# First-chunk v transposed on TensorE, q norms summed as columns, later first-chunk weight products in the out banks, opening loads reordered

## The chip, the cores and the metric

The kernel runs on one core of a Trainium2 chip. The metric is the device time of one execution in microseconds (us). A profile is one further reading of one of the timed executions; its span is about 2 us shorter than the time told for the same execution. In the profile PE is TensorE's matmuls and PEld its weight loads, DVE is VectorE, ACT is ScalarE, POOL is GpSimd and SP is SyncE. A bank is one of the buffers in PSUM into which TensorE writes its products and from which ACT or DVE empty them. A transfer has landed when its data may be used.

## The reference

Four batches of cross-covariance attention (6016 positions, 256 channels) feed a SwiGLU block with 1536 hidden units.

```python
qn = q / (norm(q, axis=1) + 1e-6)          # norms over the 6016 positions
kn = k / (norm(k, axis=1) + 1e-6)
a  = softmax(kn.transpose(0, 2, 1) @ qn / tau)      # 256 x 256 per batch
x  = (v @ a).reshape(B * N, C)
out = (silu(x @ w_gate) * (x @ w_val)) @ w_out
```

## The kernel before

The kernel never forms `v @ a`. Per batch it multiplies the attention matrix into both weight matrices (the "weight products", twelve units of 128x512 each) and then runs v through the products. v is needed with channels on the partitions, so each chunk of 512 positions is cast to bf16 in DRAM and read back through a DMA transpose (`vT`). A chunk has twelve steps: one gate product, one value product, silu, multiply. The output products of a chunk are spread over the steps of the next chunk.

Batch 0 has nothing to hide behind. Its opening loads q and k, sums the squares, forms `k^T q`, takes the softmax, makes the first four weight products and starts chunk 0, making the other eight weight products during the first four steps.

```python
def load_v(b, ci):                       # cast to DRAM, then DMA transpose
    ...
    nc.gpsimd.dma_start(out=vb[:mv, :]..., in_=v[b, cs*P:cs*P+mv, :]...)
    vT = vpool.tile([P, CH, CS * P], BF16, tag="vT")
    nc.sync.dma_start_transpose(out=vT[:, :, :mv], in_=vb[:mv, :])

def first_norm(b, t, which):             # q squares on ACT, k squares on DVE
    ...
    for s in range(pm):                  # every row of ss is the same sum
        nc.tensor.matmul(ss, ones_bf, sq[:, s, :], ...)      # 256 columns

def wp_unit(b, u, pool=psum_m, tag="misc"):      # psum_m has ONE bank
    ps = pool.tile([P, WP], FP32, tag=tag)
    for jh in range(CH):
        nc.tensor.matmul(ps, exT[:, jh, ...], src[:, jh, cols], ...)
    # even units are emptied by ACT, odd ones by DVE
    ...

# ... loads of the opening, in the order of the queue
for g, which in order: load_qk(0, g, which)      # k two groups ahead of q
load_v(*allc[0]); load_w(0); load_v(*allc[1]); load_w(1); load_w(2)
nc.gpsimd.dma_start(out=w_out_sb, ...)
...
first_softmax(0); row_sums(0)
for u in range(NFIRST): wp_unit(0, u, psum_gv, ...)     # NFIRST = 4
for gi, (b, ci) in enumerate(allc):
    for f in range(FH):
        gv_step(b, ci, f, sv)
        if gi == 0:
            for u in range(NFIRST + 2*f, min(NFIRST + 2*f + 2, len(wp_units))):
                wp_unit(0, u)
        ...
        if f == 0 and gi + VT_AHEAD < len(allc): load_v(*allc[gi + VT_AHEAD])
```

Of the kernel before, what the change touches and what calls it, by code (L numbers as in the profile page):

```python
# [17 lines left out]
def kernel(  # L18
# [61 lines left out]
    half = const.tile([P, 2 * CH], FP32)  # L80
    minus = const.tile([P, 2 * CH], FP32)
    identf = const.tile([P, P], FP32)
    warm_bf = const.tile([P, 2 * C], BF16)
    nc.vector.memset(warm_bf, 1.0)

# [21 lines left out]
    def load_v(b, ci):  # L107
# [7 lines left out]
        nc.sync.dma_start_transpose(out=vT[:, :, :mv], in_=vb[:mv, :])  # L115
        vt_ready[(b, ci)] = vT

    def gemm1_pair(b, t):

        q_sb, k_sb = qk_tiles[b]  # L120
        if t == 0:
            kq_new = psum_kq.tile([P, CH, C], FP32, tag="kq")
            state[b, "kq"] = kq_new
        kq = state[b, "kq"]
        ps, pm = pairs[t]
        last = t == NP - 1
        for jh in range(CH):
            js = slice(jh * P, (jh + 1) * P)
            if pm == 2:
                nc.tensor.matmul(kq[:, jh, :], q_sb[:, ps:ps + 2, js],  # L130
                                 k_sb[:, ps:ps + 2, :],
                                 start=(t == 0 and jh == 0), stop=last,
                                 perf_mode=DR, skip_group_check=True)
            else:
                nc.tensor.matmul(kq[:, jh, :], q_sb[:, ps, js], k_sb[:, ps, :],
                                 start=(t == 0 and jh == 0), stop=last,
                                 skip_group_check=True)

    def first_norm(b, t, which):

        x_sb = qk_tiles[b][which]
        ps, pm = pairs[t]
        sq = sqpool.tile([P, 2, C], BF16, tag="sq%d" % which)
        if which == 0:
            nc.scalar.activation(sq[:, :pm, :], x_sb[:, ps:ps + pm, :], ACT.Square)  # L145
        else:
            nc.vector.tensor_mul(sq[:, :pm, :], x_sb[:, ps:ps + pm, :],  # L147
                                 x_sb[:, ps:ps + pm, :])
        if t == 0:
            ss_new = psum_gv.tile([P, C], FP32, tag="gv"[which])  # L150
            state[b, "ss", which] = ss_new
        ss = state[b, "ss", which]
        for s in range(pm):
            nc.tensor.matmul(ss, ones_bf, sq[:, s, :],  # L154
                             start=(t == 0 and s == 0),
                             stop=(t == NP - 1 and s == pm - 1))

    def first_inv_k(b):
        nrm = work.tile([P, C], FP32, tag="nrm")
        nc.scalar.activation(nrm, state[b, "ss", 1], ACT.Sqrt)  # L160
        ink = work.tile([P, C], FP32, tag="ink")
        nc.vector.tensor_scalar_add(ink, in0=nrm, scalar1=1e-6)
        nc.vector.reciprocal(ink, ink)
        state[b, "ink"] = ink

    def first_softmax(b):
        kq, ink = state[b, "kq"], state[b, "ink"]
        nrq = work.tile([1, C], FP32, tag="nrq")
        nc.scalar.activation(nrq, state[b, "ss", 0][0:1, :], ACT.Sqrt)
        qc = psum_m.tile([P, CH], FP32, tag="misc")  # L170
        for jh in range(CH):
            nc.tensor.matmul(qc[:, jh:jh + 1], nrq[0:1, jh * P:(jh + 1) * P],
                             ones_f[0:1, 0:1], start=True, stop=True)
        keep_warm(4)
        inq = work.tile([P, CH], FP32, tag="inq")
        s_f = work.tile([P, CH, C], FP32, tag="s_f")
        nc.vector.tensor_mul(s_f[:, 0, :], kq[:, 0, :], ink)
        nc.vector.tensor_scalar_add(inq, in0=qc, scalar1=1e-6)
        nc.vector.reciprocal(inq, inq)
        if inv_tau != 1.0:  # L180
            nc.vector.tensor_scalar_mul(inq, in0=inq, scalar1=inv_tau)
        nc.vector.tensor_mul(s_f[:, 1, :], kq[:, 1, :], ink)
        exT = attn.tile([P, CH, C], BF16, tag="exT")
        for jh in range(CH):
            nc.scalar.activation(exT[:, jh, :], s_f[:, jh, :], ACT.Exp,
                                 scale=inq[:, jh:jh + 1])
        state[b, "exT"] = exT

    def norm_acc(b, t):
        q_sb, k_sb = qk_tiles[b]  # L190
# [75 lines left out]
    def row_sums(b):  # L266
        exT = state[b, "exT"]
        rs = psum_m.tile([P, CH], FP32, tag="misc")
        for ih in range(CH):
            for jh in range(CH):  # L270
                nc.tensor.matmul(rs[:, ih:ih + 1], exT[:, jh, ih * P:(ih + 1) * P],
                                 ones_bf[:, 0:1], start=(jh == 0), stop=(jh == CH - 1))
        smr = work.tile([P, CH], FP32, tag="smr")
        nc.vector.tensor_scalar_add(smr, in0=rs, scalar1=1e-9)
        nc.vector.reciprocal(smr, smr)
        Wg = attn.tile([P, CH, DFF], BF16, tag="Wg")
        Wv = attn.tile([P, CH, DFF], BF16, tag="Wv")
        state[b, "smr"], state[b, "W"] = smr, (Wg, Wv)
# [5 lines left out]

    wp_units = [(wc, w, ih) for wc in range(NWC) for w in range(2) for ih in range(CH)]

    def wp_unit(b, u, pool=psum_m, tag="misc"):

        wc, w, ih = wp_units[u]
        exT, smr = state[b, "exT"], state[b, "smr"]  # L290
        src = (w_gate_sb, w_val_sb)[w]
        dst = state[b, "W"][w]
        cols = slice(wc * WP, (wc + 1) * WP)
        ps = pool.tile([P, WP], FP32, tag=tag)
        for jh in range(CH):
            nc.tensor.matmul(ps, exT[:, jh, ih * P:(ih + 1) * P], src[:, jh, cols],  # L296
                             start=(jh == 0), stop=(jh == CH - 1))
        if u % 2 == 0:
            nc.scalar.activation(dst[:, ih, cols], ps, ACT.Copy, scale=smr[:, ih:ih + 1])
        else:  # L300
            nc.vector.tensor_scalar_mul(dst[:, ih, cols], in0=ps, scalar1=smr[:, ih:ih + 1])

    def gv_step(b, ci, f, sv):
        cs, cm = chunks[ci]
# [14 lines left out]
    class OutStage:  # L319


        def __init__(self, b, ci, sv):
            cs, self.cm = chunks[ci]
            self.sv = sv
            self.n0 = b * N + cs * P
            self.at = 0
            self.n = self.cm * FH
            self.o_ps = None

        def emit(self, count):  # L330
            for _ in range(count):
                if self.at == self.n:
                    return
                j, f = divmod(self.at, FH)
                if f == 0 and j % 2 == 0:
                    o_new = psum_o.tile([P, 2, C], FP32, tag="o")
                    self.o_ps = o_new
                nc.tensor.matmul(self.o_ps[:, j % 2, :],  # L338
                                 self.sv[:, f, j * P:(j + 1) * P],
                                 w_out_sb[:, f, :], start=(f == 0), stop=(f == FH - 1))  # L340
                self.at += 1
                if f == FH - 1 and (j % 2 == 1 or j == self.cm - 1):
                    j0 = j - j % 2
                    m = j - j0 + 1
                    o_sb = opool.tile([P, 2, C], FP32, tag="o_sb")
                    if j0 == 0:
                        nc.scalar.copy(o_sb[:, :m, :], self.o_ps[:, :m, :])  # L347
                    else:
                        nc.vector.tensor_copy(o_sb[:, :m, :], self.o_ps[:, :m, :])  # L349
                    r0 = self.n0 + j0 * P  # L350
                    nc.sync.dma_start(
                        out=out[r0:r0 + m * P, :].rearrange("(s p) c -> p s c", p=P),
                        in_=o_sb[:, :m, :])


    LOAD0, SQ0 = 10, 22
# [35 lines left out]


    NG = len(groups)
    K_AHEAD = 2
    order = []
    for g in range(NG + K_AHEAD):
        if g < NG:
            order.append((g, 1))
        if g >= K_AHEAD:  # L400
            order.append((g - K_AHEAD, 0))
    for g, which in order:
        load_qk(0, g, which)
    load_v(*allc[0])
    load_w(0)
    load_v(*allc[1])
    load_w(1)
    load_w(2)
    nc.gpsimd.dma_start(out=w_out_sb, in_=moe_w_out.rearrange("(h l) d -> l h d", l=P))
    nc.gpsimd.memset(half, 0.5)  # L410
    nc.gpsimd.memset(minus, -1.0)
    make_identity(nc, identf)
    keep_warm(10)
    for g, which in order:
        gs, gm = groups[g]
        for t in range(gs // 2, (gs + gm + 1) // 2):
            first_norm(0, t, which)
            if which == 0:
                gemm1_pair(0, t)
        if which == 1 and g == NG - 1:  # L420
            first_inv_k(0)
    first_softmax(0)
    row_sums(0)
    NFIRST = 2 * CH
    for u in range(NFIRST):
        wp_unit(0, u, psum_gv, "g" if u % 2 == 0 else "v")

    prev = None
    for gi, (b, ci) in enumerate(allc):
        sv = svpool.tile([P, FH, CS * P], BF16, tag="sv")  # L430
        for f in range(FH):
            gv_step(b, ci, f, sv)
            if gi == 0:
                for u in range(NFIRST + 2 * f, min(NFIRST + 2 * f + 2, len(wp_units))):
                    wp_unit(0, u)
            if prev is not None:
                prev.emit(prev.cm)
            if b + 1 < B:
# [40 lines left out]
```

## Time and profile before

| | before |
|---|---|
| time, first three runs | 837.96 us median, 834.86 to 839.70 |
| profiled run | 839.74 us, span 837.6 us |
| first gate product (step 0) | 46.54 us |
| step 4 (weight products done) | 63.50 us |
| chunk 1 starts | 70.41 us |

The page of the kernel before: engine, busy time, share of the span, instructions; then the TensorE clock that was granted, in tenths, for 40 equal slices of the span.

```profile
PE 807.1 (96%) x4919; PEld 489.7 (58%) x5006; DVE 550.0 (66%) x860; ACT 463.9 (55%) x827; POOL 89.9 (11%) x171
...
PEclk9959999999999999999999999999999999999999
```

TensorE is busy for 96% of the span. The idle time and the one slice at half clock both lie in the first 64 us, so that is where a change can find something.

The chain of waits of the kernel before, in order of time: start, length, what.

```profile
25.91 9.58 DMA vb<-in_v_dram
...
35.51 10.98 DMA vT<-vb
...
46.54 1.01 PE g_ps L313 x2
```

The chain goes through the load of v (landed 35.5 us) and its transpose (landed 46.5 us) to the first gate product.

The TensorE timeline of the kernel before from there: start, length, engine, line, operation, in brackets the idle time before it and what ended it.

```profile
46.54 1.01 PE L313 MATMUL g_ps<-vT,Wg 128*128 128x512 bf16 x2 [5.86 <-DMA vT<-vb]
47.34 1.06 PE L313 MATMUL v_ps<-vT,Wv 128*128 128x512 bf16 x2
48.20 1.06 PE L296 MATMUL ps<-w_gate_sb,exT 128*128 128x512 bf16 x2
50.03 1.01 PE L296 MATMUL ps<-w_gate_sb,exT 128*128 128x512 bf16 x2 [0.78 <-ACT Wg L299]
```

TensorE idled 5.86 us for the first vT. After that two matmuls of 512 columns take about 0.86 us from start to start (47.34 to 48.20), and a second weight product waits 0.78 us until ACT has emptied the only misc bank.

The table of windows of the kernel before: stretch; its length, busy time and instructions of PE; then of PEld, DVE, ACT and POOL; the granted clock; DMA share; GB/s.

```profile
20.00:30.00 10.00, 6.97 (x46) 4.78 (x46) 4.86 (x8) 4.14 (x9) 4.26 (x8) 1.00 1.12 106
...
44.00:46.00 2.00, 0.00 (x0) 0.00 (x0) 0.00 (x0) 0.00 (x0) 0.53 (x1) 0.82 1.34 179
46.00:48.00 2.00, 1.46 (x4) 0.54 (x4) 0.00 (x0) 0.41 (x1) 0.53 (x1) 0.50 1.35 183
48.00:52.00 4.00, 3.22 (x8) 0.99 (x7) 1.44 (x2) 0.94 (x3) 0.10 (x1) 0.50 1.27 189
...
60.00:64.00 4.00, 3.22 (x10) 1.15 (x10) 1.51 (x3) 1.28 (x2) 1.28 (x3) 0.71 1.10 145
```

The clock falls to half inside the wait and is back only between 60 and 64 us.

### The profile page before, as it was taken

What the parts mean: (1) busy time and instruction counts of PE and PEld (TensorE: products, weight loads), DVE (VectorE), ACT (ScalarE), POOL (GpSimd) and SP (SyncE); (2) the same over time, 40 slices, a digit from 0 to 9 for tenths busy, and PEclk for the clock granted to TensorE, in tenths of its full rate; (3) what the DMA queues carried; (4) which work ended last, traced back from release to release, by engine and by line L of the source; (5) the groups of instructions that cost most, each with busy time, mean ns of one, the idle gap of its engine ahead of it and who ended that gap; (6) DMA issues with size and microseconds to landing.
All of it is one profiled execution on the core that took longest, in us unless ns stands there. A gap on an engine that the chain in (4) does not pass through costs nothing.

```text
span 837.6 us, 13474 instructions
## 1 busy us (share of the span) xinstructions
PE 807.1 (96%) x4919; PEld 489.7 (58%) x5006; DVE 550.0 (66%) x860; ACT 463.9 (55%) x827; POOL 89.9 (11%) x171
## 2 busy tenths in 40 slices
PE   7769999999999999999999999999999999999998
PEld 4425566565565656666566556666556566566566
DVE  4526788867655688867565688876755555555554
ACT  3625777645555677755545567764554544544543
POOL 5523000024300000013320000003100000000000
PEclk9959999999999999999999999999999999999999
DMA  9999621129982111217993121114931212112101
GB/s 88 147 160 125 103 64 39 51 51 153 147 133 58 41 49 39 58 47 122 134 147 78 45 62 40 51 39 85 175 70 47 51 51 64 39 51 64 42 31 58
DMA packets 93874, 64.85 MB, mean 77 GB/s; under 512 B 53616, under 2 KB 93040, under 8 KB 93040
## 3 DMA queue, kind: packets, MB, share of 16 engines
q0 software_dynamic: 18544, 27.01, 25.4%
q1 hardware_dynamic: 75264, 36.97, 18.9%
q8 instruction: 39, 0.64, 0.3%
q14 instruction: 27, 0.22, 0.1%
HBM read 78.64 MB, written 36.96 MB: 138 GB/s over the span
## 4 chain that ended last, share of the span: by engine, by line
PE 90%; DMA 5%; issue 1%; ACT 1%; DVE 1%; POOL 1%; DVEq 0%; ACTq 0%; POOLq 0%
PE o_new L338 29%; PE v_ps L313 29%; PE g_ps L313 27%; PE ps L296 3%; DMA k_sb<-in_k_dram 2%; PE kq_new L130 2%; DMA vT<-vb 1%; DMA vb<-in_v_dram 1%; ACT sq L194 1%; DVE sv L317 1%; DVE acc_new L203 1%; POOL k_sb L103 0%; PE cs L211 0%; ACT silu L316 0%; POOL q_sb L103 0%
## 5 line engine op out<-in xcount | busy, mean ns | idle before, releaser
L317 DVE TENSOR_TENSOR sv<-silu,v_ps 128x512 bf16<-128x512 bf16 (+1 forms) x576 | 382.5, 673 | 229.3 <-ACT silu L316 217.4
L316 ACT ACTIVATE silu<-g_ps 128x512 bf16<-128x512 f32 (+1 forms) x576 | 337.5, 587 | 316.7 <-PE g_ps L313 263.4
L338 PE MATMUL o_new<-w_out_sb,sv 128*128 128x256 bf16 x2256 | 338.5, 273 | 1.6
L313 PE MATMUL v_ps<-vT,Wv 128*128 128x512 bf16 (+1 forms) x1120 | 332.4, 376 | 5.8 <-DVE sv L317 3.0
L313 PE MATMUL g_ps<-vT,Wg 128*128 128x512 bf16 (+1 forms) x1101 | 329.1, 377 | 6.0 <-DMA vT<-vb 5.9
L338 PEld LDWEIGHTS <-sv 128*128 128x128 bf16 x2256 | 220.7, 98 | 140.8
L313 PEld LDWEIGHTS <-Wv 128*128 128x128 bf16 x1152 | 113.1, 98 | 136.2 <-issue 7.6
L313 PEld LDWEIGHTS <-Wg 128*128 128x128 bf16 x1152 | 107.4, 98 | 34.6 <-issue 7.8
L203 DVE TENSOR_TENSOR acc_new<-acc_new,sq 128x512 f32<-128x512 f32 x135 | 93.3, 691 | 23.6 <-ACT sq L194 21.1
L194 ACT ACTIVATE sq<-q_sb 128x512 bf16<-128x512 fp8e5 x72 | 44.3, 615 | 0.0
L194 ACT ACTIVATE sq<-k_sb 128x512 bf16<-128x512 fp8e5 x72 | 44.1, 612 | 0.0
L130 PE MATMUL kq_new<-k_sb,q_sb 128*128 128x512 fp8e5 x184 | 42.6, 313 | 0.0
L215 POOL TENSOR_TENSOR inv<-inv,half 128x4 f32<-128x4 f32 x3 | 3.1, 1036 | 360.5 <-DVE inv L214 360.5
L347 ACT COPY o_sb<-o_new 128x512 f32<-128x512 f32 x48 | 28.1, 585 | 14.0 <-PE o_new L338 13.7
L349 DVE COPY o_sb<-o_new 128x512 f32<-128x512 f32 (+1 forms) x48 | 31.7, 661 | 3.0 <-PE o_new L338 3.0
L103 POOL DMA_DIRECT2D q_sb<-in_q_dram x48 | 26.0, 541 | 38.7 <-DMA q_sb<-in_q_dram 14.6
L103 POOL DMA_DIRECT2D k_sb<-in_k_dram x48 | 25.7, 536 | 40.3 <-DMA q_sb<-in_q_dram 18.6
L111 POOL DMA_DIRECT2D vb<-in_v_dram x48 | 24.1, 505 | 24.2 <-DMA k_sb<-in_k_dram 15.3
L154 PE MATMUL ss_new<-sq,ones_bf 128*128 128x256 bf16 x94 | 18.3, 276 | 7.8 <-DVE sq L147 5.4
L147 DVE TENSOR_TENSOR sq<-k_sb 128x512 bf16<-128x512 fp8e5 (+1 forms) x24 | 15.2, 677 | 15.1 <-DMA k_sb<-in_k_dram 15.0
L145 ACT ACTIVATE sq<-q_sb 128x512 bf16<-128x512 fp8e5 (+1 forms) x24 | 13.3, 611 | 18.5 <-DMA q_sb<-in_q_dram 14.6
L130 PEld LDWEIGHTS <-q_sb 128*128 128x256 fp8e5 x184 | 22.6, 136 | 1.1
(60 smaller groups left out, 151.5 us busy)
## 6 DMA issues: line engine op xcount, KB each, us to landing
out_dram<-o_sb SPq DMA_DIRECT2D x92, 256.0 KB, 2.4
vb<-in_v_dram POOLq DMA_DIRECT2D x44, 256.0 KB, 10.7
k_sb<-in_k_dram POOLq DMA_DIRECT2D x44, 128.0 KB, 11.2
q_sb<-in_q_dram POOLq DMA_DIRECT2D x44, 128.0 KB, 11.3
w_gate_sb<-in_moe_w_gate_dram POOLq DMA_DIRECT2D x3, 256.0 KB, 9.7
w_val_sb<-in_moe_w_val_dram POOLq DMA_DIRECT2D x3, 256.0 KB, 10.0
vT<-vb SPq DMA_TRANSPOSE x48, 3.4
w_out_sb<-in_moe_w_out_dram POOLq DMA_DIRECT2D x1, 768.0 KB, 15.8
```

The lines of the kernel that those rows point to most:

```text
L103: nc.gpsimd.dma_start(out=dst[:, gs:gs + gm, :], in_=src[b].rearrange("(p s) c -> p s c", s=NS)[:, gs:gs + gm, :])
L111: nc.gpsimd.dma_start(out=vb[:mv, :].rearrange("(p s) c -> p (s c)", s=cm), in_=v[b, cs * P:cs * P + mv, :].rearrange("(p s) c -> p (s c)" ...
L130: nc.tensor.matmul(kq[:, jh, :], q_sb[:, ps:ps + 2, js], k_sb[:, ps:ps + 2, :], start=(t == 0 and jh == 0), stop=last, perf_mode=DR, skip_ ...
L194: nc.scalar.activation(sq[:, :pm, which, :], qk_tiles[b][which][:, ps:ps + pm, :], ACT.Square)
L203: nc.vector.tensor_add(acc, acc, sq[:, s, :, :])
L296: nc.tensor.matmul(ps, exT[:, jh, ih * P:(ih + 1) * P], src[:, jh, cols], start=(jh == 0), stop=(jh == CH - 1))
L313: nc.tensor.matmul(dst[:, :mv], W[:, kk, fs], vT[:, kk, :mv], start=(kk == 0), stop=(kk == CH - 1))
L316: nc.scalar.activation(silu[:, :mv], g_ps[:, :mv], ACT.Silu)
L317: nc.vector.tensor_mul(sv[:, f, :mv], silu[:, :mv], v_ps[:, :mv])
L338: nc.tensor.matmul(self.o_ps[:, j % 2, :], self.sv[:, f, j * P:(j + 1) * P], w_out_sb[:, f, :], start=(f == 0), stop=(f == FH - 1))
L347: nc.scalar.copy(o_sb[:, :m, :], self.o_ps[:, :m, :])
L349: nc.vector.tensor_copy(o_sb[:, :m, :], self.o_ps[:, :m, :])
```

## The change

The intent is to take the wait away and to tighten the opening:

1. Chunk 0's v is loaded straight into SBUF and transposed by eight TensorE transposes during the softmax; DVE copies them out. (Chunk 0's positions are then permuted, so its output is written with another pattern.)
2. q norms are summed as columns, two one-column products per slice, so that they come out on the partitions; the last q square moves to DVE. The reciprocal of the k norms is cut into two halves, made between the last q groups.
3. The first four weight products are issued so that work starts after half of the exponentials. The other eight use the two "out" banks, idle during chunk 0, in place of the one misc bank.
4. k is loaded three groups ahead of q, not two, and both weight blocks 0 and 1 go ahead of chunk 1's v.

The diff, cut to its core:

```diff
+    def load_first_v():
+        nc.gpsimd.dma_start(
+            out=v0_sb, in_=v[0, :CS * P, :].rearrange("(p s) c -> p s c", s=CS))
+    def transpose_first_v():
+        vt_ps = psum_o.tile([P, CH, CS * P], BF16, tag="o")
+        for h in range(CH):
+            for j in range(CS):
+                nc.tensor.transpose(vt_ps[:, h, j * P:(j + 1) * P],
+                                    v0_sb[:, j, h * P:(h + 1) * P], ident)
 ...
     def first_norm(b, t, which, on_dve):
+            if which == 1:
+                nc.tensor.matmul(ss, ones_bf, sq[:, s, :], start=first, stop=last)
+            else:
+                for h in range(CH):
+                    nc.tensor.matmul(ss[:, h:h + 1], sq[:, s, h * P:(h + 1) * P],
+                                     ones_bf[:, 0:1], start=first and h == 0, stop=last, ...)
 ...
     def first_softmax(b):
-        nrq = work.tile([1, C], FP32, tag="nrq")       # root of one row,
-        ...                                            # turned by two products
+        nc.scalar.activation(inq, state[b, "ss", 0], ACT.Sqrt)
 ...
+        transpose_first_v()
+        keep_warm(4)                                   # moved down to here
+        for h in range(CH):
+            evacuate_first_v(h)
 ...
-    K_AHEAD = 2
+    K_AHEAD = 3
 ...
-    load_v(*allc[0])
+    load_first_v()
     load_w(0)
+    load_w(1)
     load_v(*allc[1])
-    load_w(1)
     load_w(2)
 ...
-                    wp_unit(0, u)
+                    wp_unit(0, u, psum_o, "o")
```

More of the change, by code (lines that the diff above doesn't have):

```diff
@@ L82 @@
     identf = const.tile([P, P], FP32)
+    ident = const.tile([P, P], BF16)
+    v0_sb = const.tile([P, CS, C], BF16)
     warm_bf = const.tile([P, 2 * C], BF16)
@@ L116, in load_v, with evacuate_first_v @@
         vt_ready[(b, ci)] = vT
+    def load_first_v():
[7 more added lines that the diff above has]
+                                    v0_sb[:, j, h * P:(h + 1) * P], ident)
+        state["vt_ps"] = vt_ps
+        vT_new = vpool.tile([P, CH, CS * P], BF16, tag="vT")
+        vt_ready[(0, 0)] = vT_new
+    def evacuate_first_v(h):
+        nc.vector.tensor_copy(vt_ready[(0, 0)][:, h, :], state["vt_ps"][:, h, :])
     def gemm1_pair(b, t):
@@ L137, in gemm1_pair, with first_norm @@
                                  skip_group_check=True)
-    def first_norm(b, t, which):
+    def first_norm(b, t, which, on_dve):
         x_sb = qk_tiles[b][which]
@@ L143, in first_norm @@
         sq = sqpool.tile([P, 2, C], BF16, tag="sq%d" % which)
-        if which == 0:
-            nc.scalar.activation(sq[:, :pm, :], x_sb[:, ps:ps + pm, :], ACT.Square)
-        else:
+        if on_dve:
             nc.vector.tensor_mul(sq[:, :pm, :], x_sb[:, ps:ps + pm, :],
                                  x_sb[:, ps:ps + pm, :])
+        else:
+            nc.scalar.activation(sq[:, :pm, :], x_sb[:, ps:ps + pm, :], ACT.Square)
         if t == 0:
-            ss_new = psum_gv.tile([P, C], FP32, tag="gv"[which])
+            ss_new = psum_gv.tile([P, CH if which == 0 else C], FP32, tag="gv"[which])
             state[b, "ss", which] = ss_new
@@ L153, in first_norm, with first_norm_k @@
         for s in range(pm):
-            nc.tensor.matmul(ss, ones_bf, sq[:, s, :],
-                             start=(t == 0 and s == 0),
-                             stop=(t == NP - 1 and s == pm - 1))
-    def first_inv_k(b):
+            first = t == 0 and s == 0
+            last = t == NP - 1 and s == pm - 1
+            if which == 1:
+                nc.tensor.matmul(ss, ones_bf, sq[:, s, :], start=first, stop=last)
+            else:
+                for h in range(CH):
+                    nc.tensor.matmul(ss[:, h:h + 1], sq[:, s, h * P:(h + 1) * P],
+                                     ones_bf[:, 0:1], start=first and h == 0, stop=last,
+                                     skip_group_check=True)
+    def first_norm_k(b):
         nrm = work.tile([P, C], FP32, tag="nrm")
@@ L162, in first_inv_k @@
         nc.vector.tensor_scalar_add(ink, in0=nrm, scalar1=1e-6)
-        nc.vector.reciprocal(ink, ink)
         state[b, "ink"] = ink
+    def first_inv_k(b, h):
+        part = state[b, "ink"][:, h * P:(h + 1) * P]
+        nc.vector.reciprocal(part, part)
     def first_softmax(b):
         kq, ink = state[b, "kq"], state[b, "ink"]
-        nrq = work.tile([1, C], FP32, tag="nrq")
-        nc.scalar.activation(nrq, state[b, "ss", 0][0:1, :], ACT.Sqrt)
-        qc = psum_m.tile([P, CH], FP32, tag="misc")
-        for jh in range(CH):
-            nc.tensor.matmul(qc[:, jh:jh + 1], nrq[0:1, jh * P:(jh + 1) * P],
-                             ones_f[0:1, 0:1], start=True, stop=True)
-        keep_warm(4)
         inq = work.tile([P, CH], FP32, tag="inq")
+        nc.scalar.activation(inq, state[b, "ss", 0], ACT.Sqrt)
         s_f = work.tile([P, CH, C], FP32, tag="s_f")
         nc.vector.tensor_mul(s_f[:, 0, :], kq[:, 0, :], ink)
-        nc.vector.tensor_scalar_add(inq, in0=qc, scalar1=1e-6)
+        nc.vector.tensor_scalar_add(inq, in0=inq, scalar1=1e-6)
         nc.vector.reciprocal(inq, inq)
@@ L182, in first_softmax @@
         nc.vector.tensor_mul(s_f[:, 1, :], kq[:, 1, :], ink)
+        transpose_first_v()
+        keep_warm(4)
+        for h in range(CH):
+            evacuate_first_v(h)
         exT = attn.tile([P, CH, C], BF16, tag="exT")
+        state[b, "exT"] = exT
+        rs = psum_m.tile([P, CH], FP32, tag="misc")
+        units = []
+        for u in range(2 * CH):
+            unit_ps = psum_gv.tile([P, WP], FP32, tag="gv"[u % 2])
+            units.append(unit_ps)
+        order = (("rs", 0), (0, 0), (1, 0), ("rs", 1), (0, 1), (1, 1),
+                 (2, 0), (2, 1), (3, 0), (3, 1))
         for jh in range(CH):
@@ L186, in first_softmax @@
                                  scale=inq[:, jh:jh + 1])
-        state[b, "exT"] = exT
+        for u, jh in order:
+            if u == "rs":
+                for ih in range(CH):
+                    nc.tensor.matmul(rs[:, ih:ih + 1], exT[:, jh, ih * P:(ih + 1) * P],
+                                     ones_bf[:, 0:1], start=(jh == 0 and ih == 0),
+                                     stop=(jh == CH - 1), skip_group_check=True)
+            else:
+                wp_matmul(b, u, jh, units[u])
+            if u == 0 and jh == 1:
+                finish_rs(b, rs)
+                wp_evacuate(b, 0, units[0])
+            elif u != "rs" and jh == 1:
+                wp_evacuate(b, u, units[u])
     def norm_acc(b, t):
@@ L272, in row_sums, with finish_rs @@
                                  ones_bf[:, 0:1], start=(jh == 0), stop=(jh == CH - 1))
+        finish_rs(b, rs)
+    def finish_rs(b, rs):
         smr = work.tile([P, CH], FP32, tag="smr")
@@ L285, with wp_matmul, wp_evacuate @@
     wp_units = [(wc, w, ih) for wc in range(NWC) for w in range(2) for ih in range(CH)]
-    def wp_unit(b, u, pool=psum_m, tag="misc"):
+    def wp_matmul(b, u, jh, ps):
         wc, w, ih = wp_units[u]
-        exT, smr = state[b, "exT"], state[b, "smr"]
-        src = (w_gate_sb, w_val_sb)[w]
+        nc.tensor.matmul(ps, state[b, "exT"][:, jh, ih * P:(ih + 1) * P],
+                         (w_gate_sb, w_val_sb)[w][:, jh, wc * WP:(wc + 1) * WP],
+                         start=(jh == 0), stop=(jh == CH - 1))
+    def wp_evacuate(b, u, ps):
+        wc, w, ih = wp_units[u]
+        smr = state[b, "smr"]
         dst = state[b, "W"][w]
         cols = slice(wc * WP, (wc + 1) * WP)
-        ps = pool.tile([P, WP], FP32, tag=tag)
-        for jh in range(CH):
-            nc.tensor.matmul(ps, exT[:, jh, ih * P:(ih + 1) * P], src[:, jh, cols],
-                             start=(jh == 0), stop=(jh == CH - 1))
         if u % 2 == 0:
@@ L301, in wp_unit @@
             nc.vector.tensor_scalar_mul(dst[:, ih, cols], in0=ps, scalar1=smr[:, ih:ih + 1])
+    def wp_unit(b, u, pool=psum_m, tag="misc"):
+        ps = pool.tile([P, WP], FP32, tag=tag)
+        for jh in range(CH):
+            wp_matmul(b, u, jh, ps)
+        wp_evacuate(b, u, ps)
     def gv_step(b, ci, f, sv):
@@ L324, in __init__ @@
             self.sv = sv
-            self.n0 = b * N + cs * P
+            pat = "(p s) c -> p s c" if (b, ci) == (0, 0) else "(s p) c -> p s c"
+            r0 = b * N + cs * P
+            self.dst = out[r0:r0 + self.cm * P, :].rearrange(pat, p=P)
             self.at = 0
@@ L349, in emit @@
                         nc.vector.tensor_copy(o_sb[:, :m, :], self.o_ps[:, :m, :])
-                    r0 = self.n0 + j0 * P
-                    nc.sync.dma_start(
-                        out=out[r0:r0 + m * P, :].rearrange("(s p) c -> p s c", p=P),
-                        in_=o_sb[:, :m, :])
+                    nc.sync.dma_start(out=self.dst[:, j0:j0 + m, :], in_=o_sb[:, :m, :])
     LOAD0, SQ0 = 10, 22
@@ L401 @@
             order.append((g - K_AHEAD, 0))
-    for g, which in order:
+    for n, (g, which) in enumerate(order):
         load_qk(0, g, which)
-    load_v(*allc[0])
+        if n == 8:
+            make_identity(nc, identf)
+            nc.gpsimd.memset(half, 0.5)
+            nc.gpsimd.memset(minus, -1.0)
+    load_first_v()
     load_w(0)
+    load_w(1)
     load_v(*allc[1])
-    load_w(1)
     load_w(2)
     nc.gpsimd.dma_start(out=w_out_sb, in_=moe_w_out.rearrange("(h l) d -> l h d", l=P))
-    nc.gpsimd.memset(half, 0.5)
-    nc.gpsimd.memset(minus, -1.0)
-    make_identity(nc, identf)
     keep_warm(10)
@@ L416 @@
         for t in range(gs // 2, (gs + gm + 1) // 2):
-            first_norm(0, t, which)
+            first_norm(0, t, which, on_dve=(which == 1 or t == NP - 1))
             if which == 0:
                 gemm1_pair(0, t)
-        if which == 1 and g == NG - 1:
-            first_inv_k(0)
+        if which == 0:
+            after_k = g - (NG - 1 - K_AHEAD)
+            if after_k == 0:
+                first_norm_k(0)
+                nc.vector.tensor_copy(ident, identf)
+            elif 1 <= after_k <= CH:
+                first_inv_k(0, after_k - 1)
     first_softmax(0)
-    row_sums(0)
     NFIRST = 2 * CH
-    for u in range(NFIRST):
-        wp_unit(0, u, psum_gv, "g" if u % 2 == 0 else "v")
     prev = None
```

## The prediction

> **What bounds the kernel now.** The page gives TensorE 96% busy and the chain of waits 90% PE; after about 64 us the kernel is a steady TensorE stream which the change leaves alone. Only the opening can move. The timeline shows it: squares, norms and q/k products until 36.2 us, softmax and the first four weight products until 40.7, then TensorE waits 5.86 us for the first vT (v landed in DRAM at 35.5; its DMA transpose took 10.98 us, to 46.5). In the table of windows the granted clock falls from 1.0 to 0.5 at about 45.6 and returns only at about 62.3. From 46.5 to 63.5 (first four steps plus eight weight products) a 512-column matmul issues every 0.43 us instead of 0.216, and TensorE also waits four times 0.78 us for ACT to empty the single misc bank. The Trainium skill (TensorE: Matmul & The Clock Gate, "What's actually happening") says that TensorE drops to half rate after an idle window of about 3.4 us; this trace agrees.
>
> **What the change does, costed.**
> 1. The first vT comes from eight PE transposes[...] and two DVE evacuations (0.6 to 0.7 each, as other 128x512 PSUM reads). They run while ACT loads the exp table (1.28 us) and computes exp (0.91), so almost nothing is added. The first gate matmul moves from 46.5 to about 40.4 us: -6.1 us.
> 2. No idle window, so no half clock. The 32 matmuls of steps 0 to 3 need 6.9 us instead of 13.7: -6.8 us.
> 3. Two out banks in place of one misc bank: four waits of 0.78 go, but the silu table load (1.28 us), hidden under the vT wait until now, comes into the open and costs about 0.8 us once: about -2.4 us. Steps 0 to 3 then take about 7.7 us; step 4 starts near 48.1 instead of 63.5.
> 4. q norm columns, the last square on DVE and k one group further ahead: ACT squares (0.575 us each) still end at about 35.4, against 35.55, and the table load still follows the last root, so exp starts at about 37.7 as before: 0 to -0.5 us.
>
> Sum -15.4 us, nearly all on the critical path. The tail and all later batches are unchanged.
>
> **What may take some back.** In the DMA view loads land every 1.3 to 1.7 us. Chunk 1's v now lands later (about 42 instead of 39.5); with an 11 us transpose its vT is there at 53 to 54, needed at about 55. Chunk 2's vT was ready at 69, needed at about 70.5. The last weight blocks land at 44 and 46, needed at 45.5 and 47.2. All just in time; I allow 0.5 us on average.
>
> **Prediction: 823 us, 80% range 818.5 to 828.5** (before 837.96). Faster by over 2% (below 821.2): 0.36; within 2%: 0.62; slower by over 2%: 0.02.
>
> **What would show it.** Right: first gate matmul at 40 to 41 us with no DMA wait before it; granted clock 1.0 from 40 to 60 us; 512-column matmuls 0.216 us apart there; step 4 near 48, chunk 1 near 55 us; everything after it the same durations, shifted by 15 us. Exp at 37.7 plus or minus 0.5.
>
> **What would make it wrong.** (a) Half clock in spite of it: one-column matmuls and transposes leave TensorE less busy between 30 and 40 us, and the gate may close; up to 6 us back. (b) A wait for vT of chunk 1 or 2, 1 to 4 us, and a cold clock after it if longer than 3.4 us. (c) Weight blocks later than 46 us. (d) The evacuations of v delaying the row-sum reciprocal on DVE, up to 1 us. (e) Better than thought: the exp starting a microsecond earlier, which would carry it past 2%.

## The result

The changed kernel took 827.09 us (median of 4 runs, 826.28 to 828.49). The kernel before took 837.44 us over 4 runs of the same rounds. The ratio is 0.9879, 95% interval 0.9846 to 0.9912. Here and below a ratio is the mean time of one kernel's runs over that of the other's of the same rounds, so not quite the ratio of the medians. The change is faster by 1.2%, inside the predicted range and in the class called likeliest (within 2%), but the gain is 10.35 us by the medians where 15 were forecast. That the time fell inside the range is partly luck: when the same kernel was run again (a_again, below), its median was 830.09 us, above the upper end of 828.5.

| | before, profiled | after, predicted | after, profiled |
|---|---|---|---|
| first gate product | 46.54 | 40.4 | 40.64 |
| step 4 | 63.50 | 48.1 | 48.39 |
| chunk 1 starts | 70.41 | 55 | 57.11 |
| span | 837.6 | | 824.3 |

The page of the changed kernel:

```profile
PE 807.3 (98%) x4970; PEld 490.0 (59%) x5057; DVE 551.0 (67%) x865; ACT 463.0 (56%) x826; POOL 90.2 (11%) x171
...
PEclk7599999999999999999999999999999999999999
```

Its chain of waits:

```profile
32.30 9.56 DMA vb<-in_v_dram
...
41.87 15.20 DMA vT<-vb
...
57.11 0.60 PE g_ps L372 x2
```

Its TensorE timeline at the starts of chunk 0 and chunk 1:

```profile
40.64 0.61 PE L372 MATMUL g_ps<-vT_new,Wg 128*128 128x512 bf16 x2
...
57.11 0.60 PE L372 MATMUL g_ps<-vT,Wg 128*128 128x512 bf16 x2 [1.65 <-DMA vT<-vb]
```

And its table of windows:

```profile
20.00:30.00 10.00, 9.53 (x61) 5.02 (x60) 5.04 (x9) 4.60 (x8) 4.48 (x9) 0.50 1.13 106
...
40.00:44.00 4.00, 3.98 (x18) 1.46 (x17) 2.31 (x4) 3.97 (x6) 1.73 (x4) 1.00 1.15 182
...
48.00:52.00 4.00, 3.95 (x19) 1.82 (x19) 3.34 (x5) 2.87 (x5) 0.00 (x0) 1.00 1.28 144
...
56.00:60.00 4.00, 2.89 (x18) 1.74 (x19) 1.39 (x3) 1.19 (x2) 1.61 (x3) 1.00 1.48 130
```

Three things are to be seen. The wait before chunk 0 is gone and the clock is full from 40 to 60 us, as intended. The wait for a vT has come back in small at chunk 1: its transpose started at 41.9 us, took 15.2 us, and TensorE waited 1.65 us; that is most of the 2.1 us by which chunk 1 came later than forecast. And there is a new stretch of half clock, in the opening, before 38.5 us. The span is 13.3 us shorter, to within 0.1 us the distance between the two starts of chunk 1 (70.41 - 57.11 = 13.30): nothing later moves.

That leaves two puzzles. The profiles differ by 13.3 us but the medians by only 10.35. And 13.3 is itself less than 15.4.

### The profile page after: what moved, and what is told of

The parts are those of the page before. It is cut to its first block, busy times and chain, and to the rows that moved or that the text cites. A ratio compares the mean times of both kernels' runs of the same rounds, so it can differ in the third digit from the quotient of the medians.

```text
span 824.3 us, 13581 instructions
## 1 busy us (share of the span) xinstructions
PE 807.3 (98%) x4970; PEld 490.0 (59%) x5057; DVE 551.0 (67%) x865; ACT 463.0 (56%) x826; POOL 90.2 (11%) x171
## 4 chain that ended last, share of the span: by engine, by line
PE 89%; DMA 6%; issue 1%; DVE 1%; ACT 1%; POOL 0%; DVEq 0%; ACTq 0%; POOLq 0%
PE o_new L400 30%; PE v_ps L372 28%; PE g_ps L372 27%; DMA k_sb<-in_k_dram 2%; DMA vT<-vb 2%; PE ps L341 2%; PE kq_new L150 2%; DMA q_sb<-in_q_dram 1%; DMA vb<-in_v_dram 1%; ACT sq L243 1%; DVE sv L376 1%; DVE acc_new L252 1%; PE cs L260 0%; POOL k_sb L105 0%; ACT silu L375 0%
## 5 line engine op out<-in xcount | busy, mean ns | idle before, releaser
L372 PE MATMUL v_ps<-vT,Wv 128*128 128x512 bf16 (+1 forms) x1097 | 323.6, 374 | 5.7 <-DVE sv L376 3.0
L372 PE MATMUL g_ps<-vT,Wg 128*128 128x512 bf16 (+1 forms) x1077 | 320.1, 375 | 1.8 <-DMA vT<-vb 1.7
L150 PE MATMUL kq_new<-k_sb,q_sb 128*128 128x512 fp8e5 x184 | 46.9, 344 | 0.0
L243 ACT ACTIVATE sq<-q_sb 128x512 bf16<-128x512 fp8e5 x72 | 44.3, 615 | 0.0
L409 ACT COPY o_sb<-o_new 128x512 f32<-128x512 f32 x48 | 28.1, 585 | 14.0 <-PE o_new L400 13.7
L166 DVE TENSOR_TENSOR sq<-k_sb 128x512 bf16<-128x512 fp8e5 (+1 forms) x24 | 15.3, 680 | 13.7 <-DMA k_sb<-in_k_dram 13.7
L169 ACT ACTIVATE sq<-q_sb 128x512 bf16<-128x512 fp8e5 x23 | 13.1, 620 | 19.5 <-DMA q_sb<-in_q_dram 19.5
L178 PE MATMUL ss_new<-sq,ones_bf 128*128 128x256 bf16 x47 | 12.7, 370 | 1.7 <-DVE sq L166 1.3
```

The costliest lines, as they stand in the source:

```text
L150: nc.tensor.matmul(kq[:, jh, :], q_sb[:, ps:ps + 2, js], k_sb[:, ps:ps + 2, :], start=(t == 0 and jh == 0), stop=last, perf_mode=DR, skip_ ...
L243: nc.scalar.activation(sq[:, :pm, which, :], qk_tiles[b][which][:, ps:ps + pm, :], ACT.Square)
L372: nc.tensor.matmul(dst[:, :mv], W[:, kk, fs], vT[:, kk, :mv], start=(kk == 0), stop=(kk == CH - 1))
L409: nc.scalar.copy(o_sb[:, :m, :], self.o_ps[:, :m, :])
```

## The experiments

All were run with five rounds, next to runs of the kernel before; each has four to six timings and one profile. "b_" is built on the kernel before, "a_" on the changed one. All gave correct results.

| run | edit | time, us: median (range) | ratio to before, 95% interval | first gate | step 4 | chunk 1 |
|---|---|---|---|---|---|---|
| b_again | none | 837.43 (834.84 to 840.04) | 1.0002, 0.9975 to 1.0028 | 46.53 | 58.85 | 65.76 |
| b_warm | dummy matmuls in the wait | 833.72 (833.39 to 833.99) | 0.9954, 0.9934 to 0.9974 | 46.57 | 57.64 | 64.55 |
| b_obank | two out banks only | 832.14 (831.05 to 832.85) | 0.9939, 0.9920 to 0.9959 | 46.30 | 55.99 | 62.89 |
| b_qcol | q norm columns only | 838.07 (834.66 to 839.66) | 1.0007, 0.9983 to 1.0031 | 46.76 | 60.63 | 67.54 |
| b_pev | PE transposes only | 828.54 (828.17 to 831.25) | 0.9897, 0.9875 to 0.9919 | 40.26 | 52.09 | 58.99 |
| a_again | none | 830.09 (826.38 to 830.94) | 0.9904, 0.9880 to 0.9929 | 40.84 | 48.60 | 57.68 |
| a_rowq | q norm rows again | 828.60 (826.02 to 830.78) | 0.9893, 0.9866 to 0.9920 | 39.90 | 47.65 | 56.98 |
| a_rowq2 | the same, repeated | 828.37 (826.13 to 829.92) | 0.9890, 0.9866 to 0.9914 | 39.93 | 47.68 | 57.48 |
| a_misc | one misc bank again | 829.03 (828.03 to 829.29) | 0.9912, 0.9899 to 0.9926 | 40.88 | 52.77 | 60.05 |
| a_vb1 | chunk 1's v loaded earlier | 824.81 (824.31 to 825.15) | 0.9864, 0.9851 to 0.9878 | 41.47 | 49.22 | 56.13 |
| a_vb12 | chunk 1's and 2's v earlier | 824.25 (823.31 to 824.60) | 0.9856, 0.9843 to 0.9870 | 40.41 | 48.16 | 55.06 |
| a_rowq_vb12 | both of these | 823.63 (823.42 to 823.77) | 0.9850, 0.9837 to 0.9864 | 39.78 | 47.52 | 54.43 |

The last three columns are read from the TensorE timeline of each run's one profile.

### b_again: what varies between runs of the kernel before?

The kernel before, unchanged.

> The kernel before, unchanged, to see what varies between its own runs (834.9 to 839.7 us so far, while the change's four runs lie within 2.2 us). Theory A (the length of the half-clock stretch of before differs from run to run[...]): the profile shows a half-clock stretch clearly other than the 16.7 us (45.6 to 62.3) seen before, and the time follows, about 0.3 us less per us of half clock. Theory B (the noise is elsewhere, in the loads or in the later stages): the same 16 to 17 us of half clock, and a difference in the span that lies somewhere else in the trace. Ratio to before 1.000 either way.

The profiled run took 835.05 us, span 832.9. Its table of windows:

```profile
44.00:48.00 4.00, 1.47 (x4) 0.55 (x4) 0.00 (x0) 0.42 (x1) 1.06 (x2) 0.50 1.35 181
48.00:52.00 4.00, 3.22 (x11) 1.06 (x10) 1.73 (x3) 1.46 (x3) 0.13 (x1) 0.79 1.26 188
52.00:56.00 4.00, 2.45 (x11) 0.96 (x10) 1.83 (x3) 1.97 (x3) 1.83 (x4) 1.00 1.09 140
```

The clock is back before 52 us here, not after 60. The clock record that the trace keeps has the half-clock stretch of the wait at 6.8 us in this run and at 17.1 us in the first profile of before. The wait is the same (5.86 us), but chunk 1 starts at 65.76 instead of 70.41, 4.65 us earlier, and the span is 4.7 us shorter. Theory A holds: the kernel before is not one time but a spread of 5 us, set by how long the clock stays down. (Between these two profiles the slope is about 0.45 us per us of half clock, not 0.3 as expected.) The other timings say the same without a profile: of 37 timings of the kernel before, the four with a mean clock of 0.998 took 834.8 to 835.1 us and the five with 0.988 or less 838.6 to 840.0. A line through all 37, wherever the half clock lay, has a slope of about 0.29. The prediction subtracted its gain from a median, but had read the gain from a profile in which the stretch was long. Against this short run the change gains only 65.76 - 57.11 = 8.65 us.

### b_warm: the clock without the wait

```diff
     for u in range(NFIRST):
         wp_unit(0, u, psum_gv, ...)
+    keep_warm(24)          # 24 dummy matmuls of 512 columns
```

> The kernel before with 24 dummy matmuls of 512 columns (5.2 us at 0.216) put into its wait for the first vT; the wait, the DMA transpose and the single misc bank stay. Theory of the prediction (the wait costs twice: itself and the half clock after it): granted clock stays 1.0 from 40 to 64 us, first gate matmul still at 46.5, steps 0 to 3 take about 10 us instead of 17 (6.9 us of matmuls plus four waits of 0.78), so 6 to 7 us faster than before. Rival (steps 0 to 3 are bound by the evacuations and the one bank, and the clock hardly matters): under 2 us faster.

The clock stayed at 1.0 and the first gate product still came at 46.57. Steps 0 to 3 took 11.07 us (about 10 were expected) instead of 16.96, a gain of 5.89 us over the long stretch. But the kernel gained only about 4 us (2.2 to 5.5 by the interval) against the mean of before, where 6 to 7 were expected: the mean of before has shorter stretches too, and against the short one of b_again (12.32 us for steps 0 to 3) the gain is only 1.25. The spread of the times fell from 5 us to 0.6, which confirms b_again from the other side. The rival (the clock hardly matters) falls.

The timeline of this run also corrects the price of the single bank. The lines of PE and the evacuations of one step and a half:

```profile
47.43 0.59 PE L296 MATMUL ps<-w_gate_sb,exT 128*128 128x512 bf16 x2
48.07 0.69 ACT L299 ACTIVATE Wg<-ps,smr 128x512 bf16<-128x512 f32 x1 [0.27 <-PE ps L296]
48.80 0.59 PE L296 MATMUL ps<-w_gate_sb,exT 128*128 128x512 bf16 x2 [0.78 <-ACT Wg L299]
...
49.43 0.75 DVE L301 TENSOR_SCALAR Wg<-ps,smr 128x512 bf16<-128x512 f32 x1 [0.91 <-PE ps L296]
...
50.24 0.59 PE L296 MATMUL ps<-w_val_sb,exT 128*128 128x512 bf16 x2
```

At full clock the bank goes round from matmul to ACT to matmul to DVE in 50.24 - 47.43 = 2.81 us per step, where the eight matmuls of a step need 8 x 0.216 = 1.73. So the bank costs about 1.1 us per step, not 0.78: with a faster array the same evacuations weigh more. The two terms of the prediction, cold clock (6.8) and bank (2.4), were priced one after the other from the same slow trace. Their sum, 9.2 us, is what was measured (16.96 - 7.75 = 9.2), but 5.9 of it is the clock and 3.3 the bank, if the clock is taken first and from the long stretch. Taken the other way round (b_obank, below, 9.69 us) the banks alone save 7.3 and the clock then 1.9, so the split is not a property of the two causes by themselves.

### b_pev: the PE transposes alone

```diff
-    load_v(*allc[0])
+    load_first_v()
 ...
+        transpose_first_v()
         keep_warm(4)
 ...
+        for h in range(CH):
+            evacuate_first_v(h)
```

(with the identity made earlier and chunk 0's output pattern, as in the change; row norms, misc bank and load order stay as before)

> The kernel before with only the PE transposes of the first v (and the identity made earlier); row norms and the single misc bank stay. Theory: first gate matmul near 40.5, no half clock, so wait and clock are both saved and only the bank waits stay: 11 to 13 us faster than before, within 1 us of the change itself, or even past it, as chunk 1 will wait for its vT in the change but, with its v loaded earlier here, not here. Rival (the double out banks or the norm columns carry a good part of the change): under 8 us faster.

The TensorE timeline of b_pev at the starts of chunk 0 and chunk 1:

```profile
40.26 0.59 PE L336 MATMUL g_ps<-vT_new,Wg 128*128 128x512 bf16 x2
...
58.99 0.59 PE L336 MATMUL g_ps<-vT,Wg 128*128 128x512 bf16 x2
```

The first gate product came at 40.26, the clock stayed full throughout the profile, chunk 1 started at 58.99 without a wait. (One of the six timings, not profiled, was 831.25 us with a mean clock of 0.994; the others lie within 0.5 us.) Ratio 0.9897 against 0.9879 and 0.9904 for the change itself. In the timelines 11.4 us are gained over the first profile of before, as expected. By the times it is 8.6 us (ratio; 6.8 to 10.5 by the interval) to 9.5 us (medians): less than the 11 to 13 expected, for the reason that b_again showed, and not enough to exclude the rival's "under 8" by the times alone. But they cannot be told from the gain of the whole change. So of the change's parts the PE transposes alone bring about what the whole brings, although the out banks save 4.1 us more in steps 0 to 3 (11.83 us here, 7.75 in the change). Where those 4 us go, a_misc and a_vb1 show.

### a_misc and b_obank: the banks

```diff
-                    wp_unit(0, u, psum_o, "o")      # a_misc; b_obank the reverse
+                    wp_unit(0, u)
```

> The changed kernel with the later weight products of the first chunk back in the single misc bank. By the two traces at full clock (before with dummy matmuls 11.07 us, transposes alone 11.83 us for steps 0 to 3, the change 7.75) the bank costs 3.3 to 4.1 us there: step 4 near 52.3, chunk 1 near 59.2. Its vT is there at 57.1, so there is no wait, and of the 4 us only about 2.1 are lost: 829.2 us. The prediction's own reckoning (four waits of 0.78 less 0.8 for the table load) says 2.4 us for steps 0 to 3, so step 4 near 50.8 and 0.7 us slower than the change.

Step 4 came at 52.77, 4.4 us later than in the change and close to the expected 52.3; the prediction's own price (50.8) falls. The time was the expected one as well (829.03 against 829.2). Yet chunk 1 started only 2.9 us later (60.05 against 57.11), and the median is within the spread of the change's. The expectation that vT would be there by 57.1 was wrong: the transpose started at 42.4 and took 17.6 us. The gain of the out banks is real in steps 0 to 3, but in the change it is partly spent waiting for chunk 1's vT, and by the times a_misc and the change are not separated (0.9899 to 0.9926 against 0.9846 to 0.9912 and 0.9880 to 0.9929).

> The kernel before with the later first-chunk weight products in the two out banks, and nothing else: the vT wait and the fall of the clock stay. Theory I (the clock stays down for 7 to 17 us after the wait because the bank waits leave gaps in the matmul stream; without gaps it returns after one or two windows of 3.4 us): clock back at 1.0 by 54 us at the latest, in the profile and in all runs, steps 0 to 3 in 9 to 11 us, 3 to 5 us faster than before, and no two groups of times. Rival J (the return of the clock has nothing to do with the gaps): half clock for up to 17 us as before, steps 0 to 3 in about 13.7 us, 2 to 3 us faster, times spread over 4 us as before.

Half clock lasted 6.8 us after the wait, steps 0 to 3 took 9.69 us, the ratio is 0.9939, about 5 us, and six runs lie within 1.8 us. That is what theory I expected, and rival J's 13.7 us did not come. A caveat: one profile of before also had only 6.8 us of half clock, so that a stream without gaps brings the clock back sooner rests on the narrow spread of the six times and of their mean clocks (0.994 to 0.996, where the 37 timings of the kernel before have 0.985 to 0.998), not on the one profile.

### b_qcol, a_rowq: the half clock in the opening

b_qcol takes the q norm columns alone into the kernel before; a_rowq takes them back out of the change.

```diff
-            nc.tensor.matmul(ss, ones_bf, sq[:, s, :], ...)
+            for h in range(CH):
+                nc.tensor.matmul(ss[:, h:h+1], sq[:, s, h*P:(h+1)*P], ones_bf[:, 0:1], ...)
```

> The kernel before with q norms as columns and nothing else. Theory C (one-column matmuls keep the clock at half once it has fallen[...]): half clock from some moment between 9 and 13 us to 30 us or later, where the kernel before and its repeat had at most 3.4 us of it. Rival D (it was the third k group ahead): full clock by 16 us. The time stays within 1 us of before either way, since the loads bound that stretch and the vT wait covers what is lost at its end.

The table of windows of b_qcol:

```profile
20.00:30.00 10.00, 9.77 (x64) 5.34 (x63) 5.17 (x8) 4.35 (x9) 4.43 (x8) 0.50 1.13 106
```

In b_qcol the clock fell at about 10 us and stayed at half for 30.7 us by the clock record; in before it was full there. Theory C holds: the columns keep it down. The mean clocks of all runs agree: 0.973 to 0.982 in the six of b_qcol, 0.988 to 0.998 in the runs of the kernel before next to them. The profile calls TensorE 98% busy in this line, so a busy TensorE in the profile doesn't mean that the clock is full; why one-column matmuls keep it down is not shown. The time did not change (1.0007), as expected: the first gate product came 0.2 us later, after a wait for vT of 4.68 us.

> The changed kernel with q norms as rows again (one 256-column matmul per slice, root of one row, two one-row products), all else as changed. Theory C (the half clock from 11.5 to 38 us in the changed kernel comes from the one-column matmuls[...]): clock 1.0 from 12 to 38 us, and the last q/k product ends near 36.2 instead of 36.7; the time is the same within 1 us, since loads bound that stretch and the exp table load hides the rest. Rival D (the half clock is chance, or comes from the k group more that is ahead): the half clock stays. Mean clock 0.99 or more under C, 0.983 under D.

The same line of a_rowq:

```profile
20.00:30.00 10.00, 7.47 (x51) 4.98 (x48) 4.97 (x9) 4.59 (x8) 4.56 (x8) 1.00 1.13 106
```

With rows in the changed kernel the clock fell too, at about 9 us, but was back after 6.8 us (3.4 us in a_rowq2), so the fall is chance (b_again and b_warm have one of 3.4 us as well) and the staying down is the columns. Again all runs agree: mean clocks of 0.992 to 1.000 in the six of a_rowq, 0.979 to 0.987 in the ten of the change. The first gate product came at 39.90, not 40.64: the columns cost 0.7 us there. None of that reached the time: chunk 1 started at 56.98, waiting 2.26 us for its vT, as late as in the change. But the six times fell into two groups, three at 826.0 to 826.8 (mean clock 0.996 to 1.000) and three at 830.4 to 830.8 (0.992 to 0.995), which no theory had foreseen.

### a_again and a_rowq2: the slow group

> a_rowq once more, unchanged, to catch a profile of its slow group if luck has it. Theory G: if the profiled run is near 830.5, its clock falls to 0.5 at or just after the wait for chunk 1's vT (54.6 to 57) for 3.4 or 6.8 us, and the matmuls of chunk 1 issue every 0.43 us there. Rival H: the clock is full there, and the 4 us are lost before 54 us or after 80. If the profiled run is near 826.5, nothing is settled.

The TensorE timeline of a_rowq2, whose profiled run is in the middle (828.3 us):

```profile
54.15 0.59 PE L371 MATMUL v_ps<-vT_new,Wv 128*128 128x512 bf16 x2
57.48 1.03 PE L371 MATMUL g_ps<-vT,Wg 128*128 128x512 bf16 x2 [2.73 <-DMA vT<-vb]
58.31 1.06 PE L371 MATMUL v_ps<-vT,Wv 128*128 128x512 bf16 x2
```

After 2.73 us of waiting the matmuls of chunk 1 issue 0.43 us apart: the clock fell to half, for 3.4 us by the clock record. That is what theory G says, though in a run of the middle; no run of a_rowq's own slow group was profiled.

> The change itself, unchanged, again, to have it in one job with the others. Time 826 to 829 us, ratio to before 0.988 within 0.003. Clock at half through most of the opening again (columns), and the wait for chunk 1's vT of about 1.7 us at 55.4 again, whichever chip it is; if the wait is absent in this run, theory E loses ground.

The repeat of the change hit the slow group in its profile (830.5 us, span 828.5). The wait at chunk 1 was 2.01 us. Its timeline at chunk 2:

```profile
73.21 0.46 PE L150 MATMUL kq_new<-k_sb,q_sb 128*128 128x512 fp8e5 x2
75.64 0.61 PE L372 MATMUL g_ps<-vT,Wg 128*128 128x512 bf16 x2 [1.97 <-DMA vT<-vb]
76.08 1.02 PE L372 MATMUL v_ps<-vT,Wv 128*128 128x512 bf16 x2
```

and windows:

```profile
76.00:77.00 1.00, 1.00 (x5) 0.36 (x3) 0.00 (x0) 0.71 (x2) 0.44 (x1) 0.56 0.98 87
77.00:78.00 1.00, 1.00 (x6) 0.66 (x5) 0.73 (x2) 0.93 (x2) 0.07 (x1) 0.50 1.75 223
```

Here TensorE waited 1.97 us more, for chunk 2's vT (loaded at 55.0 us, its transpose took 20.6), and the clock then went to half for 3.4 us. Against the first profile of the change: chunk 1 0.6 us later, chunk 2 2.5 us later (75.64 against 73.10), and about 1.7 us for 3.4 us at half clock. That is the 4.2 us between the spans. So the change has small waits for two vTs, and by chance they set off the half clock again. In the ten runs of the change four are at 829.9 us or above and six at 828.5 or below. That phase decides is argued, not shown: the stretches in the clock records are multiples of 3.4 us, and waits of nearly equal length did and did not set one off. One simple form of it does not fit: in a_again the clock changes at 4.43, 11.26, 38.57, 76.11 and 79.53 us, whole steps of 3.41 us apart, and if these steps are continued the wait of 2.01 us (55.67 to 57.68) and that of 1.97 us (73.67 to 75.64) each lie within one step, yet only the second was followed by half clock.

### a_vb1, a_vb12, a_rowq_vb12: the load order

```diff
     load_w(0)
+    load_v(*allc[1])       # a_vb1, as in the kernel before
     load_w(1)
-    load_v(*allc[1])
     load_w(2)
+    load_v(*allc[2])       # a_vb12 too; not again in chunk 0
```

> The changed kernel with one order of loads changed back: chunk 1's v before the second weight block, as in the kernel before. Theory E (what was lost is the wait for chunk 1's vT alone): its transpose starts near 39.3 instead of 41.9 and lands near 49 to 51, chunk 1 starts at 55.4 instead of 57.1 without a wait, and the kernel is 1.7 us faster than the change, about 825.4 us. Rival F (the transposes are late as a row, so the next one takes the gain back): chunk 1 starts at 55.4 all the same, but chunk 2's vT still lands near 73, TensorE waits 1.5 to 2 us for it there, and the time is that of the change within 0.5 us.

Chunk 1's transpose started at 39.5 us and took 9.6 us instead of 15.2, and there was no wait at chunk 1 (56.13, with a first gate product that came late at 41.47) nor at chunk 2. The lines of the transpose in the change and in a_vb1 (last column: us from issue to landing), then chunk 1's start in a_vb1:

```profile
vT<-vb SPq DMA_TRANSPOSE x1, 15.2
...
vT<-vb SPq DMA_TRANSPOSE x1, 9.6
...
56.13 0.59 PE L372 MATMUL g_ps<-vT,Wg 128*128 128x512 bf16 x2
```

Median 824.81, within 0.9 us. Its interval (0.9851 to 0.9878) overlaps the change's first and lies just below its second, and the two ran in different jobs, so that it is faster rests on the missing waits in the traces as much as on the times. Theory E came nearest; rival F failed at one point: chunk 2's v did not stay late. The DMA view shows what came earlier with it. The line of the output weights in the changed kernel:

```profile
w_out_sb<-in_moe_w_out_dram POOLq DMA_DIRECT2D x1, 768.0 KB, 18.3
```

and in a_vb1:

```profile
w_out_sb<-in_moe_w_out_dram POOLq DMA_DIRECT2D x1, 768.0 KB, 14.5
```

The output weights, issued at about 36 us in both, landed nearly 4 us sooner, and chunk 2's v behind them 14.4 us after its issue instead of 17.8. That the earlier transpose made room for them is argued, not shown. The Trainium skill (DMA: Bandwidth & Descriptors, "Issuing engines are not separate DMA queues") says that DMAs from all queues run on the same 16 engines and interleave. The times agree: the same 256 KB transpose has a median of 3.4 us over the kernel before and took 9.4 (b_pev) to 17.6 us (a_misc) for chunk 1. That it is the output weights in particular that slow it was not tested by itself, and they cannot be all of it: chunk 3's transpose in the change, issued at 58.9 us after they had landed, took 24.7, in part beside chunk 2's.

> As a_vb1, and chunk 2's v is loaded before the output weights too. Both transposes then land early (chunk 1 near 50, chunk 2 near 60 us). No wait for a vT at chunk 1 or 2: chunk 1 starts near 55.4, chunk 2 near 71.0, 1.7 to 2.0 us faster than the change (about 825.2). What could spoil it: the output weights land 1.3 to 1.7 us later (near 55.5 instead of 54), and the first output product of chunk 1 wants them at 56.2.

No wait for a vT, chunk 1 at 55.06, no wait for the output weights either. Median 824.25, ratio 0.9856. That is about half a microsecond better than a_vb1, which the intervals do not separate; moving chunk 1's load alone already takes both waits away.

> The candidate for the best: a_vb12 with q norms as rows again. Theory C says that the clock is then full from about 16 us on at the latest, so the first gate matmul comes at 39.9 instead of 40.6 as in a_rowq, chunk 1 at about 54.7, chunk 2 at 70.3: 2.4 to 2.6 us faster than the change, about 824.6. Theory G (the slow half of a_rowq's runs, 830.4 to 830.8 against 826.0 to 826.8, is a half clock set off in some runs by its 2.3 us wait for chunk 1's vT): no runs 4 us above the others here, spread under 1.5 us. Rival H (the two groups come from the opening): the two groups stay, 4 us apart.

```profile
54.43 0.59 PE L371 MATMUL g_ps<-vT,Wg 128*128 128x512 bf16 x2
```

First gate product at 39.78, chunk 1 at 54.43 without a wait, 823.63 us; four runs within 0.4 us. Rival H falls and theory G is what is left: without the waits the two groups are gone, here and in the eight runs of a_vb1 and a_vb12, where the kernels with waits (the change and a_rowq, with their repeats) had 8 of 22 timings at 829.9 us or above. Waits for a vT may not be the only cause: the one slow timing of b_pev had none in its kernel's profile. This version beats both kernels: it is 1.5% faster than before, and its slowest run (823.77) is below the fastest of the change's ten (826.28), though those ran in other jobs. Of the ratios, its interval lies clear of the change's second (0.9880 to 0.9929) and overlaps the first. It is not separated from a_vb12. Not tested by themselves were the third k group ahead, the last q square on DVE and the earlier start of the first four weight products.

## Why the prediction was right or wrong

- **What bounds the kernel; only the opening moves.** Right. The spans differ by 13.3 us, as the starts of chunk 1 do.
- **First gate product at 40.4.** Right: 40.64, and 40.26 with the PE transposes alone. No DMA wait before it.
- **No half clock after 40 us, 6.8 us saved; bank and table load, 2.4 us.** Right in sum (step 4 at 48.39, predicted 48.1), wrong in the parts: with the clock taken first 5.9 us are the clock's and 3.3 the bank's, with the banks first 1.9 and 7.3. The bank cost about 1.1 us a step at full clock, not the 0.78 read at half clock.
- **Exp at 37.7, norms worth 0 to -0.5.** The exp did start as before (37.79 us against 37.74; with rows again, at 37.40). The norm columns cost 0.7 us at the first gate product, because risk (a) came true: half clock in the opening. It was named at up to 6 us.
- **"What may take some back ... I allow 0.5 us on average."** This term failed. The prediction saw that chunk 1's v now lands later and that chunk 2's vT had little room, but gave the transpose the 11 us that it had taken in an earlier place. It took 15.2 us. The trace of before held a warning that was overlooked: chunk 2's transpose, issued there at 52.8 us, took 16.2. The wait was 1.65 to 2.0 us at chunk 1, in some runs 1.97 at chunk 2, and then, in those, a window of 3.4 us at half clock, which costs about 1.7. Taking the waits away (a_vb12) gives 824.25 us, close to the 823 forecast.
- **A cold clock "if longer than 3.4 us".** Too lenient: waits of 1.97 and 2.73 us were each followed by one.
- **The base.** The gain was read from the one profile of before (839.74 us) and subtracted from a median (837.96). b_again shows that profile to be at the long end: the gain in the traces is 13.3 us against it and 8.65 against a short run. The 10.35 us of the medians lie between.
- **The chances.** "Within 2%" at 0.62 was the right favourite. Even the best version, without any wait, reaches 1.5%, so 0.36 for over 2% was high. And the range held by luck in part: the first four runs of the change had a median of 827.09 us, the next six 830.09, outside it, because four of the six fell in the slow group.

## What to carry to other kernels

When a change removes a wait, everything behind it comes early, so work out each later transfer's landing again with the neighbours it will now have, not with the duration it had elsewhere; a load moved back by one place let in waits of 1.65 to 2.01 us here, and in some runs half clock after them. Where a wait also lets the clock fall, its price varies from run to run: look at the spread of the times and at more than one profile before subtracting a gain from a median. And two costs in one loop (clock and bank) are not to be priced one after the other from the slow trace: the faster one makes the other dearer.

## What the Trainium skill lacked or had wrong

- TensorE: Matmul & The Clock Gate ("What's actually happening") gives the half clock after at least one idle window of about 3.4 us. Waits of 1.97 us (a_again) and 2.73 us (a_rowq2) were followed by it, while 2.01 us earlier in a_again was not. The stretches themselves are indeed multiples of its window: 3.4, 6.8, 17.1 and 27.3 us in the clock records.
- The same page gives the full clock back after at least one sustained busy window of about 3.4 us; it has no figure for how soon it returns in a stream with short gaps. Here it took 17.1 us in one run of the kernel before, TensorE being 80% busy by the profile (3.22 of 4 us), and 6.8 us in another.
- The page says nothing of one-column matmuls and the clock: with them, in b_qcol, the clock stayed at half for 30.7 us with TensorE 98% busy by the profile.
- Its Part 4 gives about 275 to 390 ns for one 128x128 transpose, and no figure for several in a row. One lasted 0.22 us at full clock (b_pev) and 0.31 us at half clock (the change) by the profile, whose ends are modelled; in a row they started 0.055 and 0.107 us apart, so that eight took 0.62 and 1.06 us.
- DMA: Bandwidth & Descriptors has no figure for a DMA transpose among other loads: 256 KB took 9.4 to 17.6 us for chunk 1 in these runs, against a median of 3.4 us in the whole kernel before.
